# A linear-attention layer and two expert layers on one core: another order for products, weight decoding and attention pieces

## Chip, cores and metric

The kernel runs on one core of a Trainium2 chip. The metric is the device time of one execution, in microseconds (us), as the median of several runs. The engines are named as the profile names them: PE (TensorE, matmuls; PEld is its weight loads), DVE (VectorE), ACT (ScalarE), POOL (GpSimd) and SP (the queue that issues most transfers). Each works through its own instructions in the order in which they were written; they wait for each other by semaphores.

## Reference

Three layers follow each other. The first is a gated linear attention with a state per head (batch 4, 8 heads, 768 positions, 48 wide); the other two are dense layers on its output, with 3072 tokens of 384 numbers.

```
for t in range(S):                       # attention, per batch b and head h
    cur = einsum('bhd,bhe->bhde', u * k[t], v[t])
    y[t] = einsum('bhd,bhde->bhe', r[t], state + cur)
    state = w[t][..., None] * state + einsum('bhd,bhe->bhde', k[t], v[t])
h = x @ w_in;  g = h * clip(h + 3, 0, 6) / 6;  x = g @ w_out       # d_ff 2048
out = ((x @ w_a) * (x @ w_b)) @ w_out2                             # d_ff 1536
```

## The kernel before, in words

The 768 positions are cut into six blocks of 128. A **unit** is one block of one batch: units 0 to 23, four to a block, so units 12 to 23 are blocks 3 to 5 (counted from 0). The attention of a unit is a row of small pieces, each with a letter: on DVE the scans `z`, `c`, `s` over the decays, then `k` (r and k scaled by them); on PE the transposes `T` (copied out by ACT, `t`) and the products `A` (masked on DVE, `m`); the products `K`, which the state update `e`, `f`, `h` on DVE takes; the output `Y`, added up on DVE (`x`); and the transposes `X`, which `H` on ACT and `L` on DVE split into a high and a low part for the next layer. POOL prepares two products `d` per unit, DVE reduces them (`o`), POOL applies them (`O`).

The first dense layer goes over the blocks in **steps** of one weight tile `f` (16 to a block). Step s has one group of nine matmuls `h` (`L1_pe`), and on ACT and DVE `relu`, the product `mul`, the high part `gh` and the low part `gl` (`L1_relu`, `L1_mul`, `L1_high`, `L1_low`); two steps later nine matmuls into `x2a` (`L2_pe`). Blocks 0 and 1 are computed in two halves of eight tiles each, so that steps 8 to 15 are block 1's first half, 16 to 23 block 0's second, 24 to 31 block 1's second. Where a half ends, ACT and DVE copy the three `x2a` banks out (`x2e`), and the next half's first `x2a` product needs these banks. Later layers (`L3_pe`, `L4_pe`, matmuls `ab` and `oa`) follow in the same manner.

Weights come as raw 64-bit words and are **decoded** on the core, a tile of 128x768 at a time: ACT scales the high and the low word (`w_scale_h`, `w_scale_l`), DVE shifts and sets signs (`w_shift`, `w_sign`), POOL adds the halves (`w_add`), and then ACT writes the high part and DVE the low part (`w_split`, `w_high`, `w_low`). Raw tiles have two buffers: the load of a tile waits until POOL has added the tile two before.

Nothing plans the order: it is written out. `run` goes through the steps; in each it issues the attention's vector pieces that are due (`att_ew`), the step's matmuls and vector work, the decoding, and last the attention's PE pieces (`att_pe`). Which piece is due in which step stands in `CFG`: `off` and `second` give a unit's first step n0, and `stage` the steps after it. PSUM has eight banks; attention takes 5, 6, 7 in rotation:

```
    def att_bank(kind, n):
        if ring["use"]:
            i = ring["use"].pop(0)
        else:
            i = (5, 6, 7)[ring["i"] % 3]
            ring["i"] += 1
```

`T`, `A` and `X` take one bank each, `K` and `Y` two.

Of the kernel before, what the change touches and what calls it, by code (L numbers as in the profile page):

```python
# [36 lines left out]

CFG = {
    "off": (0, 3, 6, 9),
    "stage": (0, 1, 2, 3, 4, 5, 0, 2),  # L40
    "second": (17, 20, 23, 26),
    "dec": (8, 9, 11, 12, 14, 15, 18, 19),
    "late": (-16, -14, -12, -10, -8, -6, -4, -2, -1, 0, 1, 2, 3, 4, 5, 6, 7, 8),
    "heat": 13,
    "pool": (
# [27 lines left out]
def rwkv_moe_kernel(ctx: ExitStack, tc: tile.TileContext, rkw, nat, vst, wall, ub, ud, cst, out):  # L73
# [304 lines left out]
    def att_ew(n, stage):  # L378
        j = units[n][0]
        for a in {  # L380
            0: "zcs", "d0": "d", "d1": "oO", 1: "ku" if j else "k", 2: "tm",
            3: "efh" if j < NBLK - 1 else "ef", "x": "x", 5: "HL",
        }.get(stage, ""):
            atom[a](n)

    def att_pe(n, stage):
        for a in {1: "TA", 2: "K", 3: "Y", 4: "X"}.get(stage, ""):
            atom[a](n)

    def heat(k, s):  # L390
# [57 lines left out]
    def w_dec(i):  # L448
        if wide:
            w_scale_l(i)  # L450
            w_shift(i)
            w_sign(i)
            for q in range(2):
                w_add(i, q, nc.gpsimd)
# [69 lines left out]

    def L1_ew(s):
        L1_relu(s)
        L1_mul(s)

    def L1_ew2(s):
        L1_high(s)  # L530
        L1_low(s)

# [79 lines left out]
    def L4_pe(s):  # L612
        j, f = divmod(s, NF2)
        if f == 0:
            acc2[j] = [bank(i, None, f"oa{j}_{i}") for i in (0, 1, 2, 5)]
        ph, pl = G.pop(("b", s))
        w = W[NF1 + NF2 + f // 2]
        c = (f % 2) * 384
        wh, wl = w[:, 0, c:c + 384], w[:, 1, c:c + 384]
        last = f == NF2 - 1  # L620
        seq = [(b, lt, rt) for b in range(B) for lt, rt in ((ph, wh), (ph, wl))] + [(b, pl, wh) for b in range(B)]
        if s == NBLK * NF2 - 1:
            seq.sort(key=lambda x: x[0])
        for b, lt, rt in seq:
            nc.tensor.matmul(  # L625
                out=acc2[j][b][:, 0:384], lhsT=lt[:, b * 128:(b + 1) * 128], rhs=rt,
                start=(f == 0 and rt is wh and lt is ph), stop=(last and lt is pl),
            )
        for b in range(B):
            o = acc2[j][b][:, 0:384]  # L630
            if f == NF2 - 1:
                if b < 3:
                    e = ap_.tile([128, 3 * DM], F32, name=f"oe{j}_{b}", tag="nat", bufs=3)
                else:
                    e = ap_.tile([128, NP * 112], F32, name=f"oe{j}_{b}", tag="kt", bufs=1)
# [188 lines left out]
    def run(at, first, ew, fast):  # L824
        lag, end = [max(first - 1, 0), 0], NA + NBLK * NF2 - 1
        for s in range(first, end + 1):
            act = at.get(s, [])
            sb = s - NA
            for n, sg in act:
                ew(n, sg)  # L830
            if 0 <= s < NA:
                L1_pe(s)
            elif 0 <= sb < NBLK * NF2:
                L3_pe(sb)
            if 0 <= s < NA:
                L1_ew(s)
                L1_ew2(s)
            elif 0 <= sb < NBLK * NF2:
                L3_ew(sb)
            w_step1(s)  # L840
            w_step(s)
            while lag[0] <= min(s - 2, NA - 1):
                L2_pe(lag[0])
                lag[0] += 1
# [52 lines left out]
    with tc.manual_schedule():  # L897
# [90 lines left out]
```

## Time and profile before

| what | value |
|---|---|
| runs shown | 1016.33, 1019.26, 1019.84 us; median 1019.26 |
| profiled execution | 1015.68 us, its span on the core 1013.9 us |
| PE busy | 993.1 us (98%) |
| DVE, ACT, POOL busy | 587.8 (58%), 345.7 (34%), 122.1 us (12%) |
| mean granted TensorE clock | 0.990 of full speed |

The profiled execution is the one that the traces show; it is a little faster than the three runs. A busy share is a mean over stages: PE is full for most of the time, and the few places where it is not are named in the rows below.

### The profile page before, as it was taken

Reading aid. Unit: us, or ns where it says so; the run is one execution under the profiler, and the core shown is the slowest. Engines: PE = TensorE matmul, PEld = TensorE weight load, DVE = VectorE, ACT = ScalarE, POOL = GpSimd, SP = SyncE. Lnnn points to the kernel's source line nnn. Section 1 sums busy time; section 2 is a strip of 40 time slices with the busy share of each in tenths; the row PEclk is TensorE's granted clock in tenths of the full one; section 3 lists DMA queues with packets and bytes.
Section 4 is the critical chain, followed back from the end, with each engine's and each line's share of the span. In section 5 each row is a group of like instructions: output and inputs, shape, how many; then the busy total and the mean of one; then the engine's idle time right before and its main releaser. Section 6 shows DMA issues by size and latency. Waiting matters only on the chain.

```text
span 1013.9 us, 16923 instructions
## 1 busy us (share of the span) xinstructions
PE 993.1 (98%) x7146; PEld 817.2 (81%) x7146; DVE 587.8 (58%) x916; ACT 345.7 (34%) x578; POOL 122.1 (12%) x119
## 2 busy tenths in 40 slices
PE   9999988999999999999999999999999999999997
PEld 5777766787878777777888888888888888888886
DVE  7997787757656765663677673444444444444222
ACT  4464653333223323232566552222222222222211
POOL 1230323111211120210222330000000000000000
PEclk9999989999999999999999999999999999999999
DMA  7362532332231321220243440110110110110001
GB/s 289 132 236 71 209 102 102 118 127 71 87 103 55 103 87 63 95 102 1 94 155 125 159 164 1 56 42 22 65 41 23 64 44 23 63 42 14 32 1 35
DMA packets 30037, 86.64 MB, mean 85 GB/s; under 512 B 3456, under 2 KB 10880, under 8 KB 29952
## 3 DMA queue, kind: packets, MB, share of 16 engines
q1 hardware_dynamic: 29664, 85.37, 24.5%
q8 instruction: 58, 0.95, 0.4%
q14 instruction: 27, 0.22, 0.1%
q10 hardware_dynamic: 288, 0.10, 0.0%
HBM read 74.45 MB, written 11.01 MB: 84 GB/s over the span
## 4 chain that ended last, share of the span: by engine, by line
PE 89%; DVE 6%; DMA 2%; issue 2%; ACT 1%; SPq 0%; DVEq 0%; ACTq 0%
PE ab L474 30%; PE h L474 19%; PE x2a L543 18%; PE oa L625 15%; PE A L272 2%; PE Y L339 2%; DMA rkw<-in_rkw_dram 1%; PE K L294 1%; DVE raw L435 1%; PE T L251 1%; PE X L356 1%; DVE w L464 1%; DVE zp L184 1%; DVE rkw L206 1%; DVE t L513 1%
## 5 line engine op out<-in xcount | busy, mean ns | idle before, releaser
L474 PE MATMUL ab<-xh_b,w 128*128 128x512 f32 x864 | 225.6, 396 | 0.0
L474 PEld LDWEIGHTS ab<-xh_b,w 128*128 128x128 f32 x864 | 161.7, 188 | 33.2
L543 PE MATMUL x2a<-gh,w 128*128 128x512 f32 x576 | 156.7, 403 | 6.2 <-ACT x2e L562 5.5
L603 DVE TENSOR_TENSOR ta<-ab,ta 128x512 f32<-128x512 f32 x72 | 49.7, 691 | 187.9 <-PE ab L474 187.8
L474 PE MATMUL h<-xh_a,w 128*128 128x512 f32 x576 | 157.7, 409 | 0.6 <-ACT xh_a L364 0.6
L543 PEld LDWEIGHTS x2a<-gh,w 128*128 128x128 f32 x576 | 108.9, 191 | 34.4 <-ACT x2e L562 6.3
L509 ACT ACTIVATE t<-h,half 128x512 f32<-128x512 f32 x96 | 65.9, 686 | 181.8 <-PE h L474 181.7
L474 PEld LDWEIGHTS h<-xh_a,w 128*128 128x128 f32 x576 | 105.0, 190 | 25.0 <-ACT xh_a L364 0.8
L474 PE MATMUL ab<-xl_b,w 128*128 128x512 f32 x432 | 124.4, 396 | 0.0
L625 PE MATMUL oa<-w,ph 128*128 128x384 f32 x576 | 113.7, 338 | 0.0
L513 DVE SCALAR_TENSOR_TENSOR t<-t,h 128x512 f32<-128x512 f32 x96 | 65.3, 680 | 79.2 <-ACT t L509 78.8
L522 DVE TENSOR_TENSOR gl<-t,gh 128x512 fp32r<-128x512 f32 x96 | 74.9, 780 | 60.6 <-ACT gh L517 60.6
L625 PEld LDWEIGHTS oa<-w,ph 128*128 128x128 f32 x576 | 103.2, 188 | 6.0
L606 ACT CAST ph<-ta 128x512 fp32r<-128x512 f32 x72 | 44.7, 621 | 160.8 <-DVE ta L603 160.8
L602 ACT COPY ta<-ab 128x512 f32<-128x512 f32 x72 | 42.1, 585 | 164.7 <-PE ab L474 164.7
L474 PEld LDWEIGHTS ab<-xl_b,w 128*128 128x128 f32 x432 | 81.4, 188 | 20.1
L517 ACT CAST gh<-t 128x512 fp32r<-128x512 f32 x96 | 59.5, 620 | 106.4 <-DVE t L513 106.4
L442 POOL TENSOR_TENSOR wa<-wa,raw 128x384 int32<-128x384 int32 x60 | 65.2, 1106 | 198.5 <-DVE raw L435 152.5
L543 PE MATMUL x2a<-gl,w 128*128 128x512 f32 x288 | 86.8, 401 | 0.0
L474 PE MATMUL h<-xl_a,w 128*128 128x512 f32 x288 | 83.3, 397 | 0.0
L607 DVE TENSOR_TENSOR pl<-ta,ph 128x512 fp32r<-128x512 f32 x72 | 54.0, 750 | 49.4 <-ACT ph L606 49.4
L543 PEld LDWEIGHTS x2a<-gl,w 128*128 128x128 f32 x288 | 55.0, 191 | 13.5
(86 smaller groups left out, 1023.0 us busy)
## 6 DMA issues: line engine op xcount, KB each, us to landing
raw<-in_wall_dram SPq DMA_DIRECT2D x34, 768.0 KB, 4.3
rkw<-in_rkw_dram SPq DMA_DIRECT2D x21, 772.5 KB, 4.9
nat<-in_nat_dram SPq DMA_DIRECT2D x16, 576.0 KB, 3.8
cw<-in_rkw_dram SPq DMA_DIRECT2D x24, 260.5 KB, 2.7
x2d<-x2e SPq DMA_DIRECT2D x18, 256.0 KB, 2.1
x2r<-x2d SPq DMA_DIRECT2D x18, 256.0 KB, 3.1
out_dram<-oe SPq DMA_DIRECT2D x24, 192.0 KB, 2.0
vs<-in_vst_dram SPq DMA_DIRECT2D x22, 192.0 KB, 5.0
```

The lines of the kernel that those rows point to most:

```text
L442: eng.tensor_tensor(out=a[:, c], in0=a[:, c], in1=t[:, c, 0], op=ALU.add)
L474: nc.tensor.matmul(out=o, lhsT=lt, rhs=rt, start=(i == 0), stop=(i == 3 * n - 1))
L509: nc.scalar.activation(out=t, in_=hb[s], func=ACTF.Relu, bias=half, scale=1.0 / 6.0)
L513: nc.vector.scalar_tensor_tensor(out=t, in0=t, scalar=1.0, in1=hb.pop(s), op0=ALU.min, op1=ALU.mult)
L517: nc.scalar.copy(out=gh, in_=G["t", s])
L522: ve(f"l{s}").tensor_tensor(out=gl, in0=G.pop(("t", s)), in1=G[s][0].bitcast(F32), op=ALU.subtract)
L543: nc.tensor.matmul(out=acc1[i][k][:, c0:c1], lhsT=w[:, e, 384 + k * 128:512 + k * 128], rhs=rt, start=(first and e == 0 and rt is gh), sto ...
L602: nc.scalar.copy(out=t, in_=a)
L603: nc.vector.tensor_tensor(out=t, in0=bb, in1=t, op=ALU.mult)
L606: nc.scalar.copy(out=gh, in_=t)
L607: nc.vector.tensor_tensor(out=gl, in0=t, in1=gh.bitcast(F32), op=ALU.subtract)
L625: nc.tensor.matmul(out=acc2[j][b][:, 0:384], lhsT=lt[:, b * 128:(b + 1) * 128], rhs=rt, start=(f == 0 and rt is wh and lt is ph), stop=(la ...
```

## The change

It does six things.
1. In the first dense layer, DVE's product `mul` stands ahead of the shift of a weight tile, ACT's scaling of the high word stands between `relu` and `gh`, and the shift between `mul` and `gl`.
2. The tiles 8 to 15 are decoded in steps 8, 9, 10, 12, 13, 14, 16, 17 (before: 8, 9, 11, 12, 14, 15, 18, 19), and up to step 23 each is split one step after its decoding and not two.
3. The scans of unit 8, and in blocks 3 to 5 those of the second to fourth unit of a block, are issued behind the step's product and not ahead of it.
4. In blocks 3 to 5 a unit's `Y` stands one step later, in the step of the next unit's `T` and `A`, and its `X` in the step of the next unit's `K`. The PE pieces of such a step are sorted T, t, Y, A, K, X.
5. `d` of a unit is prepared earlier: two steps in block 2, one in blocks 3 to 5.
6. At the end, the last output tile is copied and sent in two halves by DVE with SP and by ACT, the first of the four goes through ACT's queue, and the flag that decides on the general path is read three steps after it is made, not behind the last output.

```
-    "stage": (0, 1, 2, 3, 4, 5, 0, 2),
+    "stage": (0, 1, 2, 3, 3, 4, 4, 5, 0, 2),
+    "merged": (0, 1, 2, 3, 4, 5, 5, 6, -1, 2),
-    "dec": (8, 9, 11, 12, 14, 15, 18, 19),
+    "dec": (8, 9, 10, 12, 13, 14, 16, 17),
...
+    MERGED = range(12, len(units))
...
-    def att_pe(n, stage):
-        for a in {1: "TA", 2: "K", 3: "Y", 4: "X"}.get(stage, ""):
+    def att_pe(act):
+        seq = [(a, n) for n, sg in act for a in {1: "TtA" if n in MERGED else "TA", 2: "K", 3: "Y", 4: "X"}.get(sg, "")]
+        if any(n in MERGED for a, n in seq):
+            seq.sort(key=lambda x: "TtYAKX".index(x[0]))
+        for a, n in seq:
             atom[a](n)
...
     def L1_ew(s):
         L1_relu(s)
+        w_step1(s)
         L1_mul(s)
-
-    def L1_ew2(s):
+        w_step1b(s)
         L1_high(s)
         L1_low(s)
...
+                if end and b == B - 1:
+                    c = DM // 2
+                    nc.vector.tensor_copy(out=e[:, 0:c], in_=o[:, 0:c])
+                    nc.sync.dma_start(out=out[r0:r0 + 128, 0:c], in_=e[:, 0:c])
+                    nc.scalar.copy(out=e[:, c:DM], in_=o[:, c:DM])
+                    nc.scalar.dma_start(out=out[r0:r0 + 128, c:DM], in_=e[:, c:DM])
+                    continue
...
+    def w_step1b(s):
+        if wide:
+            for i in wdue(s):
+                w_shift(i)
...
-        while pend and pend[0][0] <= s - 2:
+        while pend and pend[0][0] <= s - (1 if s < F0 + NF1 else 2):
...
+            behind = [x for x in act if fast and x[1] == 0 and (x[0] == FIRST_N or x[0] in MERGED and x[0] % 4)]
             for n, sg in act:
-                ew(n, sg)
+                if (n, sg) not in behind:
+                    ew(n, sg)
...
+            if fast and sb == CHECK + 3:
+                chk["good"] = nc.values_load(chk["flag"][0:1, 0:1], min_val=0, max_val=128)
             w_step2(s)
-            for n, sg in act:
-                att_pe(n, sg)
+            for n, sg in behind:
+                ew(n, sg)
+            att_pe(act)
```

**ACT, steps 9 and 10.** `t9` is `relu` of step 9, `raw9` the scaling of tile 9, `w8` the high part of tile 8, `x2e` the copies of the banks. Before:

```order
L509 ACTIVATE t9_1447<-h9_1437,half_85 128x512
L517 CAST gh9_1450<-t9_1447 128x512
L417 ACTIVATE raw9_1435<-raw9_1435 128x768
L562 COPY x2e0_1464<-x2a0_0_929 128x512
L562 COPY x2e0_1464<-x2a0_2_931 128x512
L426 ACTIVATE raw9_1435<-raw9_1435 128x768
L509 ACTIVATE t10_1489<-h10_1479,half_85 128x512
L517 CAST gh10_1492<-t10_1489 128x512
L461 CAST w8_1496<-wa8_1430 128x768
```

With the change:

```order
L513 ACTIVATE t9_1447<-h9_1437,half_85 128x512
L422 ACTIVATE raw9_1435<-raw9_1435 128x768
L521 CAST gh9_1453<-t9_1447 128x512
L465 CAST w8_1457<-wa8_1425 128x768
L566 COPY x2e0_1469<-x2a0_0_929 128x512
L566 COPY x2e0_1469<-x2a0_2_931 128x512
L431 ACTIVATE raw9_1435<-raw9_1435 128x768
L513 ACTIVATE t10_1492<-h10_1482,half_85 128x512
L422 ACTIVATE raw10_1480<-raw10_1480 128x768
L521 CAST gh10_1498<-t10_1492 128x512
```

The high part of tile 8 has moved ahead of the copies, and a scaling ahead of each `gh`; tile 10 is scaled in step 10.

**DVE, steps 17 and 18**, where the first half of block 1 ends and unit 8 begins. `t17` is the product of step 17, `zp8` the two scans of unit 8, `rkw8` its `k`. Before:

```order
L184 SCALAR_TENSOR_TENSOR zp8_1718<-rkw8_1511,ones_rev_87 128x520
L192 TENSOR_SCALAR pc8_1720<-zp8_1718 128x8
L193 RECIPROCAL seed_88<-pc8_1720 128x8
L197 SCALAR_TENSOR_TENSOR zp8_1718<-rkw8_1511,seed_88 128x519
L513 SCALAR_TENSOR_TENSOR t17_1736<-t17_1736,h17_1726 128x512
L522 TENSOR_TENSOR gl17_1741<-t17_1736,gh17_1739 128x512
L464 TENSOR_TENSOR w13_1743<-wa13_1682,w13_1743 128x768
L560 COPY x2e1_1755<-x2a1_1_1500 128x512
L206 TENSOR_TENSOR rkw8_1511<-rkw8_1511,zp8_1718 128x1024
```

With the change:

```order
L517 SCALAR_TENSOR_TENSOR t17_1742<-t17_1742,h17_1732 128x512
L436 TENSOR_SCALAR wa15_1746<-raw15_1730 128x768
L526 TENSOR_TENSOR gl17_1750<-t17_1742,gh17_1748 128x512
L468 TENSOR_TENSOR w14_1752<-wa14_1711,w14_1752 128x768
L564 COPY x2e1_1764<-x2a1_1_1506 128x512
L440 SCALAR_TENSOR_TENSOR raw15_1730<-raw15_1730 128x768
L186 SCALAR_TENSOR_TENSOR zp8_1775<-rkw8_1523,ones_rev_87 128x520
L194 TENSOR_SCALAR pc8_1777<-zp8_1775 128x8
L195 RECIPROCAL seed_88<-pc8_1777 128x8
L199 SCALAR_TENSOR_TENSOR zp8_1775<-rkw8_1523,seed_88 128x519
L208 TENSOR_TENSOR rkw8_1523<-rkw8_1523,zp8_1775 128x1024
```

The scans have moved from ahead of the product to behind the copy and the sign of tile 15, and `k` now stands directly behind them.

**DVE, steps 38 and 39**, unit 14 in block 3, as in all second to fourth units of blocks 3 to 5. `t38` is the product of step 38, `gl38` its low part, `zp14` the scans, `rkw14` the `k` for which `T` of unit 14 waits at the end of step 39, `nat13` the `x` of unit 13. Before:

```order
L184 SCALAR_TENSOR_TENSOR zp14_2927<-rkw14_2807,ones_rev_87 128x520
L192 TENSOR_SCALAR pc14_2929<-zp14_2927 128x8
L193 RECIPROCAL seed_88<-pc14_2929 128x8
L197 SCALAR_TENSOR_TENSOR zp14_2927<-rkw14_2807,seed_88 128x519
L513 SCALAR_TENSOR_TENSOR t38_2945<-t38_2945,h38_2935 128x512
L522 TENSOR_TENSOR gl38_2950<-t38_2945,gh38_2948 128x512
L349 TENSOR_TENSOR nat13_2407<-Y0_13_2961,nat13_2407 128x4x48
L349 TENSOR_TENSOR nat13_2407<-Y1_13_2962,nat13_2407 128x4x48
L206 TENSOR_TENSOR rkw14_2807<-rkw14_2807,zp14_2927 128x1024
```

With the change:

```order
L517 SCALAR_TENSOR_TENSOR t38_2939<-t38_2939,h38_2929 128x512
L526 TENSOR_TENSOR gl38_2944<-t38_2939,gh38_2942 128x512
L186 SCALAR_TENSOR_TENSOR zp14_2955<-rkw14_2860,ones_rev_87 128x520
L194 TENSOR_SCALAR pc14_2957<-zp14_2955 128x8
L195 RECIPROCAL seed_88<-pc14_2957 128x8
L199 SCALAR_TENSOR_TENSOR zp14_2955<-rkw14_2860,seed_88 128x519
L208 TENSOR_TENSOR rkw14_2860<-rkw14_2860,zp14_2955 128x1024
L311 TENSOR_TENSOR sp14_0_2962<-st2_95,pc14_2957 112x192
L517 SCALAR_TENSOR_TENSOR t39_2974<-t39_2974,h39_2964 128x512
L526 TENSOR_TENSOR gl39_2979<-t39_2974,gh39_2977 128x512
```

The scans have moved from ahead of `t38` to behind `gl38`. On PE, before, step 38 ends with `Y` of unit 13, and step 39 with `X` of unit 13 and `T`, `A` of unit 14; now step 38 ends with its `x2a` products alone, step 39 with `T` of 14, `Y` of 13, `A` of 14, and step 40 with `K` of 14 and `X` of 13.

## Rows read from the trace of the kernel before

**Rows 1.** Waits of PE: waiting engine and line, releaser, us in total, times, longest.

```profile
PE x2a L543 <- ACT x2e L562: 5.5, 2, 3.7
```

**Rows 2.** Stretches: us, busy time of each engine, granted clock (PEclk), DMA.

```profile
147.84:153.20 5.36, 5.36 (x17) 3.72 (x19) 4.31 (x8) 3.30 (x6) 0.00 (x0) 0.50 0.77 275
173.75:177.10 3.35, 3.35 (x17) 2.62 (x14) 2.71 (x4) 1.21 (x3) 0.44 (x1) 0.52 0.00 0
```

**Rows 3.** Timeline, steps 8 to 10: start, us, engine, instruction, [idle before <- releaser].

```profile
103.19 0.91 ACT L417 ACTIVATE raw<-raw 128x768 f32<-128x768 f32 x1 [0.68 <-DMA raw<-in_wall_dram]
...
105.99 1.99 POOL L442 TENSOR_TENSOR wa<-wa,raw 128x384 int32<-128x384 int32 x2 [24.19 <-DVE raw L435]
...
107.85 1.05 ACT L562 COPY x2e<-x2a 128x512 f32<-128x512 f32 x2
...
108.47 2.79 PE L543 MATMUL x2a<-gh,w 128*128 128x512 f32 x6 [1.80 <-ACT x2e L562]
```

**Rows 4.** Timeline, steps 17 and 18, DVE and PE.

```profile
141.57 2.05 DVE L184 TENSOR_TENSOR_SCAN zp<-rkw,ones_rev 128x520 f32<-128x520 f32 x1
...
144.10 1.24 DVE L197 TENSOR_TENSOR_SCAN zp<-rkw,seed 128x519 f32<-128x519 f32 x1
...
147.84 3.19 PE L543 MATMUL x2a<-gh,w 128*128 128x512 f32 x6 [3.67 <-ACT x2e L562]
...
152.10 0.95 PE L251 MATMUL T<-cst_sb,rkw 112*128 112x112 f32 x4
```

**Rows 5.** Timeline, end of step 21, DVE and PE.

```profile
171.06 1.22 DVE L206 TENSOR_TENSOR rkw<-rkw,zp 128x1024 f32<-128x1024 f32 x1
...
172.38 0.57 PE L251 MATMUL T<-cst_sb,rkw 112*128 112x112 f32 x4 [3.17 <-issue]
```

**Rows 6.** Page, DMA issues: transfer, queue, count, KB each, median us to landing.

```profile
raw<-in_wall_dram SPq DMA_DIRECT2D x34, 768.0 KB, 4.3
```

**Rows 7.** Timeline of PE in block 3's steps.

```profile
228.61 1.57 PE L474 MATMUL h<-xh_a,w 128*128 128x512 f32 x6
...
232.83 1.57 PE L474 MATMUL h<-xh_a,w 128*128 128x512 f32 x6
...
248.04 0.33 PE L339 MATMUL Y<-sp,rkw 48*64 48x48 f32 x8
...
249.12 1.67 PE L474 MATMUL h<-xh_a,w 128*128 128x512 f32 x6
...
253.76 0.55 PE L251 MATMUL T<-cst_sb,rkw 112*128 112x112 f32 x4
...
255.32 1.67 PE L474 MATMUL h<-xh_a,w 128*128 128x512 f32 x6
```

**Rows 8.** Timeline of ACT and DVE behind the `h` that starts at 255.32.

```profile
257.79 0.69 ACT L509 ACTIVATE t<-h,half 128x512 f32<-128x512 f32 x1 [2.86 <-PE h L474]
...
259.24 0.62 ACT L517 CAST gh<-t 128x512 fp32r<-128x512 f32 x1 [0.76 <-DVE t L513]
...
259.89 0.69 DVE L522 TENSOR_TENSOR gl<-t,gh 128x512 fp32r<-128x512 f32 x1 [0.69 <-ACT gh L517]
```

**Rows 9.** Timeline of DVE and ACT, scans, `k`, state scale and `t` of one unit.

```profile
244.91 1.23 DVE L184 TENSOR_TENSOR_SCAN zp<-rkw,ones_rev 128x520 f32<-128x520 f32 x1
...
246.62 1.24 DVE L197 TENSOR_TENSOR_SCAN zp<-rkw,seed 128x519 f32<-128x519 f32 x1
...
250.26 1.21 DVE L206 TENSOR_TENSOR rkw<-rkw,zp 128x1024 f32<-128x1024 f32 x1
...
251.39 0.35 DVE L309 TENSOR_TENSOR sp<-st,pc 112x192 f32<-112x192 f32 x1
...
254.40 0.53 ACT L261 COPY kt<-T 128x448 f32<-128x448 f32 x1
```

**Rows 10.** Instructions of line 905, the reading of the flag: ns, start in us.

```profile
L905 PEldq TENSOR_LOAD <-chk_flag x1: 487/487/487, 1004.0 to 1004.0; - x1
...
L905 SPq TENSOR_LOAD <-chk_flag x1: 565/565/565, 1008.5 to 1008.5; - x1
```

More of the change, by code (lines that the diff above doesn't have):

```diff
@@ L380, in att_ew @@
         for a in {
-            0: "zcs", "d0": "d", "d1": "oO", 1: "ku" if j else "k", 2: "tm",
-            3: "efh" if j < NBLK - 1 else "ef", "x": "x", 5: "HL",
+            0: "zcs", "d0": "d", "d1": "oO", 1: "ku" if j else "k", 2: "m" if n in MERGED else "tm",
+            "e": "efh" if j < NBLK - 1 else "ef", "x": "x", 5: "HL",
         }.get(stage, ""):
             atom[a](n)
-    def att_pe(n, stage):
-        for a in {1: "TA", 2: "K", 3: "Y", 4: "X"}.get(stage, ""):
+    def att_pe(act):
[3 more added lines that the diff above has]
+        for a, n in seq:
             atom[a](n)
@@ L450, in w_dec @@
             w_scale_l(i)
-            w_shift(i)
             w_sign(i)
@@ L637, in L4_pe @@
                 r0 = b * S + j * 128
+                end = s == NBLK * NF2 - 1
+                if end and b == B - 1:
[5 more added lines that the diff above has]
+                    continue
                 if b % 2 == 0:
@@ L641, in L4_pe @@
                     nc.vector.tensor_copy(out=e, in_=o)
-                nc.sync.dma_start(out=out[r0:r0 + 128, :], in_=e)
+                (nc.scalar if end and b == 0 else nc.sync).dma_start(out=out[r0:r0 + 128, :], in_=e)
     at = {}
-    STAGES = (0, 1, 2, 3, "x", 4, 5, "d0", "d1")
+    STAGES = (0, 1, 2, "e", 3, "x", 4, 5, "d0", "d1")
     for n in range(FIRST_N, len(units)):
@@ L648, in rwkv_moe_kernel @@
         n0 = CFG["second"][i] if j == 2 else NF1 * (j - 1) + CFG["off"][i]
-        a, b, c, d, x, h, d0, d1 = (n0 + k for k in CFG["stage"])
+        p = [n0 + k for k in CFG["merged" if n in MERGED else "stage"]]
         if j == 2:
-            h = max(h, F0 + NF1)
-        for sg, s in zip(STAGES, (a, b, c, d, x, h - 1, h, d0, d1)):
+            p[7] = max(p[7], F0 + NF1)
+            p[6] = p[7] - 1
+            p[8] -= 2
+        for sg, s in zip(STAGES, p):
             at.setdefault(s, []).append((n, sg))
     for s in at:
-        at[s].sort(key=lambda x: (x[0], {"d1": 3.5, "d0": 0.5, "x": 3.7}.get(x[1], x[1])))
+        at[s].sort(key=lambda x: (x[0], {"e": 2.5, "d1": 3.5, "d0": 0.5, "x": 3.7}.get(x[1], x[1])))
     wdec = {}
@@ L836, in run @@
                 L1_ew(s)
[L837 to L840, printed above, removed]
+            elif s < 0:
+                w_step1(s)
+                w_step1b(s)
+            else:
+                if 0 <= sb < NBLK * NF2:
+                    L3_ew(sb)
+                w_step1(s)
             w_step(s)
+            if s >= NA:
+                w_step1b(s)
             while lag[0] <= min(s - 2, NA - 1):
@@ L904, in rwkv_moe_kernel @@
         run(at, F0, att_ew, True)
-        good = nc.values_load(chk["flag"][0:1, 0:1], min_val=0, max_val=128)
-        with tc.If(good < 128):
+        with tc.If(chk["good"] < 128):
             general_attention()
```

## Prediction

> **What bounds the kernel now.** The page's busy times come first: PE is busy for 993.1 of 1013.9 us, so an edit is worth what it takes from PE's own row or from the few places where PE stands still. The waits of PE name the largest, the first `x2a` product of a half, which waited for ACT's copies of the banks [rows 1]. The timeline gives the places. There are three stops, all in steps 10 to 21: 1.80 us at 108.47 [rows 3], 3.67 at 147.84 [rows 4] and 3.17 at 172.38 [rows 5]. After each the granted clock is at its lower level, 1.2 GHz, for a while: 0.50 of full speed over 5.36 us after the second, 0.52 over 3.35 us after the third [rows 2]. So the second stop costs 3.67 + 5.36 / 2 = 6.3 us and the third 3.17 + 3.35 / 2 = 4.8 us; the first at least 1.80 + 2.79 - 1.57 = 3.0, by its first six matmuls beside six at full clock [rows 3, 7]. From there to the end PE is full. In blocks 3 to 5 a step without attention takes 232.83 - 228.61 = 4.22 us, and an `h` behind attention pieces shows 1.67 us for its first six matmuls where a plain one shows 1.57: returning from small pieces costs 0.10 us [rows 7]. The kernel has little to win: the stops of blocks 0 and 1, about 14 us, the 0.10s, and the tail.
>
> **Blocks 3 to 5, second to fourth unit (9 units).** This is where the sum is decided. `T` of such a unit comes two steps behind the `h` of its first step; call the start of that `h` zero. PE reaches `T` after a step behind attention pieces, 4.32 us, and a plain one, 4.22: at 8.54 [rows 7]. On the other side DVE must finish `k`, and the scans that `k` needs now stand behind `gl` of the first step. `relu` starts at 257.79 - 255.32 = 2.47, `gl` 2.10 later at 4.57, and ends at 5.26 [rows 8]. From the first scan's start to the end of the second are 246.62 + 1.24 - 244.91 = 2.95 us: 8.21. `k` takes 1.21: 9.42 [rows 9]. The only row in which `T` waited for `k` has `k` end at 171.06 + 1.22 = 172.28 and `T` start 0.10 later [rows 5]. So `T` starts at 9.4 to 9.5, and PE stands still for **0.95 us**; the lower figure holds if each instruction starts a little before its forerunner's end, as `k` and the state scale do (251.39 is 0.08 before 250.26 + 1.21 [rows 9]). Before, the scans ran while PE made the first `h`, and no `T` of this stretch shows a wait.
>
> A second wait follows. A step's pieces now take banks in the order T, Y, Y, A out of three, so `A` gets `T`'s bank and must wait for `t`, ACT's copy. `t` stands behind `gh` of the same step, whose product stands on DVE behind `k` and the state scale. From the end of `k` at 9.42: state scale 0.35 [rows 9], then from the product's start to `gh` 259.24 - 257.79 - 0.69 = 0.76 us, `gh` 0.62 [rows 8], `t` 0.53 [rows 9]: 11.7, or 11.4 with the small overlaps. PE meanwhile does `T`, 0.55, and `Y`, 249.12 - 248.04 = 1.08 [rows 7]: 9.5 + 1.6 = 11.1. So `A` waits for 0.3 us (0.2 to 0.6). Before, `X`, `T`, `A` stood in three different banks. Together 0.95 + 0.3 = 1.25 us per unit, times nine: **+11.3 us**. The bounds are +7 (the overlaps cut the first wait to 0.8 and `A` finds its bank free) and +14. Behind PE's wait nothing else is late: `h` of the next step has its bank, and the next unit's chain starts from its own `h`, so the wait does not grow and is not made up.
>
> The rows show `T` and the following `h` without a wait bracket where the banks rotate [rows 7]. The Trainium skill (Perfetto Trace Analysis, Matmuls) says that independent groups should rotate through different PSUM banks, so that the copy of one runs beside the next group's matmuls; this change breaks that for `T` and `A`. By the rule alone `A` would wait for all of `t`, less the `Y` between them, which gives the same sum to within the bounds above.
>
> **What the grouping gives back.** A block's attention stood in 13 groups on PE and now in 10, so three returns of 0.10 us are saved per block: **-0.9 us** in three blocks, -1.8 if entering a group costs as much. No matmul is removed.
>
> **Blocks 0 and 1.** The edits go both ways here.
> First stop: the copies started at 107.85 [rows 3]; now the high part of tile 8 stands ahead of them, and it needs POOL's adds. These ended at 105.99 + 1.99 = 107.98, and they come about 0.5 us later, since ACT waits until 103.19 for the raw tile [rows 3] with `gh` now behind that wait. High part 0.9 (the row of the same size on ACT, 0.91 [rows 3]): copies at 109.3 or so, **+1.4 us**.
> Second stop: unit 8's scans no longer hold up the product, so the copies could come earlier. But `k` of unit 8 now follows the copy, the sign, and both scans: the scans took 144.10 + 1.24 - 141.57 = 3.77 us beside POOL [rows 4], `k` 1.22 [rows 5], together 4.99, while PE has one half step of 2.11 us to do. From those alone `T` waits for 2.9 us, and for up to 4.3 with the copy and the sign at 0.69 each (the nearest row, `gl` [rows 8]). The stop moves from `x2a` to `T`; I take 4.0, **+0.3 us**.
> Three tiles in four steps: a raw tile's load starts when POOL has added the tile two before and takes 4.3 us to land [rows 6]. From there ACT's two scalings and a high part (0.9 each), `gh` 0.6, DVE's sign about 0.7 and the adds 1.99 make 10.3 us for two tiles, 5.2 a tile. The steps ask for one every 4 x 4.22 / 3 = 5.6. So there is no slack to make up the first stop's lateness, and ACT, with `gh` behind the scaling, hands each late load on to the copies of the next half: 0 to 5 us later. I take 3.2, half of the range and some clock with it, **+3.2 us**.
> Third stop: decoding is done by then and no sign stands in front of unit 9's scans, so `T` of unit 9 finds `k` done: 3.17 + 1.7 = 4.8 us gone, **-4.9 us** with rounding.
> The sum of these four is 1.4 + 0.3 + 3.2 - 4.9 = 0, with bounds of -5 and +5.
>
> **Tail.** The flag's reading leaves SP's path behind the last transfer, 0.57 us [rows 10], and half an output tile is copied in less time, 0.2 at a guess from its halved width: **-0.8 us**, between 0 (the last landing sets the end) and -1.5. In its new place the reading takes PE's sequencer 0.49 us; before, that was done at 1004.0 while matmuls ran until 1007 [rows 10], so it hides behind queued matmuls, at 0 to +0.5.
>
> **Sum.** 0 + 11.3 - 0.9 - 0.8 = **+9.6 us**. The profiled execution took 1015.68, which gives 1025.3. It is the fastest of the four executions shown; their mean is 1017.8, and a median of new runs should lie near that plus the sum: **1027.4 us**.
>
> **Rivals.**
> A. The wait at `T` doesn't form: PE stays behind DVE. It would need `k` 0.9 us earlier, which is the point from which it decides. Against it: each link is a row, and DVE takes nothing out of order in any of them. Price: 11.3 us, leaving about -1.7: 1016, no change.
> B, the other side. The stops of blocks 0 and 1 vanish altogether, because the loads land early enough for the copies to be out when PE comes, and `T` of unit 8 finds `k` done. The point is the landing of tiles 13 and 15 before their step's `relu` ends. Price: the second stop's 6.3 and the third's 4.8 go, with nothing put in their place: -11.1, with +11.3 - 0.9 - 0.8: -1.5, so 1016, not slower. Against it: 4.99 us of DVE work stand between the copies and `T`, and PE has 2.11.
> C. The nine waits bring the clock down. Each spell like the third stop's costs 1.7 us, nine of them 15 us more: 1043. Against it: the stops that the clock followed were of 1.80 us and more [rows 3 to 5], these are 0.95 and 0.3. The Trainium skill (TensorE: Matmul & The Clock Gate, A second HAM failure mode) describes this: frequent small idles between matmul groups make the clock swing. No row here shows it for idles as short as these.
>
> **Chances.** Forecast, +4 to +16 us: 0.64. A 0.14, B 0.10, C 0.12. About 5 us, 0.5%, is what a measurement of this kernel can tell from no change. A and B end near 1016 with spreads of some 5 us, so they give most of "same" and half of "faster"; the forecast's lower edge lies at "same". That makes faster 0.11, same 0.18, slower 0.71. The likeliest case's own range is 1020 to 1034. For 8 in 10 the range reaches into A and B below and into part of C above: 1013 to 1038.
>
> **What would show it.** In the new profile, PE rows `T` of units 13, 14, 15, 17, 18, 19, 21, 22, 23 with an idle of about 0.9 us released by `k`, and `A` behind with 0.2 to 0.6 released by `t`; rounds of three steps in block 3 longer by about 1.1 us; the first stop longer, a stop at unit 8's `T`, none at unit 9's. If `T` shows no idle there, the main term is wrong (A); if the granted clock shows half speed in blocks 3 to 5, C is right.

## The result, and the profile after

| what | before | after |
|---|---|---|
| median of the runs | 1018.28 us (4 runs, 1016.33 to 1019.84) | 1031.88 us (4 runs, 1030.88 to 1032.02) |
| profiled execution, its span | 1015.68, 1013.9 us | 1030.88, 1029.1 us |
| PE busy | 993.1 us (98%) | 995.3 us (97%) |
| mean granted TensorE clock | 0.990 | 0.985 |

The changed kernel is slower: the ratio of the times is 1.0135, with a 95% interval of 1.0115 to 1.0155. PE does the same work in a longer span, so the question is where it stands still. The first view is the waits of PE after the change (microseconds in all, times, longest); it answers to [rows 1].

```profile
PE T L253 <- issue: 10.9, 10, 3.8
PE x2a L547 <- ACT x2e L566: 7.3, 2, 3.8
...
PE A L274 <- ACT kt L263: 2.3, 9, 0.3
```

`T` waits ten times where it waited once, and `A` nine times where it never did. "issue" is how the page names `T`'s releaser; the rows below show that it is `k`. They are the timeline of block 3 after the change, for the second unit: PE first, then DVE, then ACT (start, length, instruction, and in brackets the idle before it; this idle is called the bracket below). They answer to [rows 7 to 9].

```profile
248.77 1.67 PE L478 MATMUL h<-xh_a,w 128*128 128x512 f32 x6
...
256.61 0.87 PE L547 MATMUL x2a<-gl,w 128*128 128x512 f32 x3
258.27 0.57 PE L253 MATMUL T<-cst_sb,rkw 112*128 112x112 f32 x4 [0.79 <-issue]
...
259.62 0.30 PE L341 MATMUL Y<-vs,am 64*64 64x48 f32 x8
260.17 1.15 PE L274 MATMUL A<-rkw 48*64 48x64 f32 x32 [0.25 <-ACT kt L263]
...
253.34 0.69 DVE L526 TENSOR_TENSOR gl<-t,gh 128x512 fp32r<-128x512 f32 x1 [0.69 <-ACT gh L521]
253.95 1.24 DVE L186 TENSOR_TENSOR_SCAN zp<-rkw,ones_rev 128x520 f32<-128x520 f32 x1
...
256.94 1.23 DVE L208 TENSOR_TENSOR rkw<-rkw,zp 128x1024 f32<-128x1024 f32 x1
...
259.59 0.53 ACT L263 COPY kt<-T 128x448 f32<-128x448 f32 x1
```

The scans start behind `gl` at 253.95, so `k` ends at 256.94 + 1.23 = 258.17, and `T` starts 0.10 later. `t` ends at 259.59 + 0.53 = 260.12, and `A`, in the same bank, starts 0.05 later.

The stages are compared by the starts of `h` rows, which mark a place in the program: the `h` of steps 7, 16, 24 and 32, and the first `ab`, with which the later layers begin. The stretch from step 32 to the first `ab` is called blocks 3 to 5, since the attention of these blocks lies in it. The bounds of the windows are those starts (columns: stretch, its length, PE busy with the count, granted clock, share of the DMA engines, GB/s). Before:

```profile
91.34:133.47 42.13, 39.76 (x224) 0.96 0.47 169
133.47:186.32 52.85, 46.01 (x413) 0.90 0.23 83
...
228.61:547.19 318.58, 318.58 (x2709) 1.00 0.25 86
```

After the change, and below it the stretch of low clock behind the second `x2a` stop:

```profile
93.54:138.15 44.61, 39.86 (x223) 0.96 0.44 160
138.15:191.46 53.31, 46.01 (x412) 0.87 0.24 83
...
233.76:561.85 328.09, 318.66 (x2710) 1.00 0.25 83
...
151.65:165.30 13.65, 9.15 (x50) 0.50 0.37 131
```

So the profiled pair differs by +2.20 us up to step 7, where no edit acts, +2.48 in steps 7 to 15 (44.61 - 42.13), +0.46 in steps 16 to 23, nothing in steps 24 to 31, **+9.51 in blocks 3 to 5**, nothing in the later layers, and +0.54 from PE's last matmul to the end (7.08 against 6.54): 15.2 us in all, which is 1030.88 - 1015.68. Blocks 3 to 5 lose at a granted clock of 1.00, the 2.4 GHz level, and PE's own rows take as long as before (318.66 for 318.58): these are waits alone.

The rows of steps 9 to 21 after, on PE and then POOL and ACT, answer to [rows 3 to 5].

```profile
112.68 0.74 PE L547 MATMUL x2a<-gh,w 128*128 128x512 f32 x2 [3.81 <-ACT x2e L566]
...
152.39 3.19 PE L547 MATMUL x2a<-gh,w 128*128 128x512 f32 x6 [3.53 <-ACT x2e L566]
...
160.62 0.98 PE L253 MATMUL T<-cst_sb,rkw 112*128 112x112 f32 x4 [3.77 <-issue]
...
179.06 0.55 PE L253 MATMUL T<-cst_sb,rkw 112*128 112x112 f32 x4
...
108.99 2.29 POOL L447 TENSOR_TENSOR wa<-wa,raw 128x384 int32<-128x384 int32 x2 [24.99 <-DVE raw L440]
...
111.31 0.83 ACT L465 CAST w<-wa 128x768 fp32r<-128x768 f32 x1 [1.15 <-POOL wa L447]
112.05 1.06 ACT L566 COPY x2e<-x2a 128x512 f32<-128x512 f32 x2
```

The first stop grew from 1.80 to 3.81 us, the second stayed (3.53 for 3.67), a new one came at unit 8's `T`, and unit 9's `T` no longer waits.

### The profile page after: what moved, and what is told of

Its sections match the earlier page's. It is cut to its first block, busy times and chain, and to the rows that moved or that the text cites. A ratio compares the mean times of both kernels' runs of the same rounds, so it can differ in the third digit from the quotient of the medians.

```text
span 1029.1 us, 16948 instructions
## 1 busy us (share of the span) xinstructions
PE 995.3 (97%) x7146; PEld 819.2 (80%) x7146; DVE 589.0 (57%) x916; ACT 346.8 (34%) x579; POOL 123.4 (12%) x119
## 4 chain that ended last, share of the span: by engine, by line
PE 79%; DVE 9%; issue 4%; DMA 3%; ACT 3%; POOL 1%; SPq 0%; ACTq 0%; POOLq 0%; DVEq 0%
PE ab L478 29%; PE h L478 15%; PE oa L629 15%; PE x2a L547 14%; DMA raw<-in_wall_dram 2%; PE A L274 2%; DVE zp L199 2%; DVE t L517 1%; DVE zp L186 1%; POOL wa L447 1%; PE K L296 1%; PE Y L341 1%; DVE raw L440 1%; DVE gl L526 1%; DMA rkw<-in_rkw_dram 1%
```

## The experiments

The time up to step 7 changes from run to run though no edit changes the work of PE, ACT, DVE or POOL there: the `h` of step 7 starts between 91.34 and 98.27 us in the fourteen profiles. Medians of few runs therefore scatter by some 3 us, and the main measure is the table, worked out as above: microseconds longer than the profiled execution of before, stage by stage, and the time from the end of PE's last matmul row to the end of the span (read to 0.1 us).

| kernel | steps 7 to 15 | 16 to 23 | blocks 3 to 5 | last matmul to end | median, runs |
|---|---|---|---|---|---|
| changed | +2.48 | +0.46 | +9.51 | 7.08 | 1031.88, 4 |
| e1_blocks01_only | +3.14 | +0.37 | 0.0 | 6.79 | 1022.66, 10 |
| e2_scans_ahead | +2.19 | +0.44 | -1.51 | 6.97 | 1020.03, 10 |
| e3_blocks35_only | +0.17 | -0.42 | +9.52 | 6.38 | 1025.86, 4 |
| e4_t_twice | +3.20 | +0.30 | +15.66 | 6.16 | 1038.62, 4 |
| e5_stops_freed | +0.52 | +1.59 | 0.0 | 6.37 | 1019.58, 10 |
| e6_split_behind_copies | +1.49 | +3.21 | +9.51 | 7.23 | 1032.06, 2 |
| e7_old_decode_steps | +3.12 | -2.17 | +9.47 | 7.26 | 1029.84, 2 |
| e8_freed_and_scans_ahead | +0.09 | +1.63 | -1.64 | 6.72 | 1018.14, 10 |
| e9_fewer_tiles_at_ends | -3.77 | -6.20 | -1.65 | 6.66 | 1007.54, 4 |
| e10_same_old_order | -3.67 | -1.17 | -1.64 | 6.42 | 1011.63, 4 |
| e11_copies_first | -3.77 | -6.18 | -1.66 | 6.40 | 1009.02, 4 |
| e12_with_new_tail | -3.77 | -5.05 | -1.61 | 7.08 | 1010.13, 4 |

The kernel before, run beside them, had medians of 1018.1 to 1019.5. The first two columns have a scatter of their own. The changed kernel, e1, e2 and e4 do the same in steps 7 to 15 and differ by 1.0 us there. e9 and e12 do the same in steps 16 to 23 and differ by 1.2: e9 keeps a granted clock of 1.00 there behind idles of 1.06 and 1.72 us, e12 shows 0.96 over the same steps behind 1.04 and 1.70. Blocks 3 to 5 repeat to 0.05 us among kernels with the same order there.

### Which part carries the loss (e1 to e4)

**e1_blocks01_only**, against the changed kernel:

```
-    MERGED = range(12, len(units))
+    MERGED = ()
```

> The changed kernel with blocks 3 to 5 as before; the new order of blocks 0 and 1 and the new tail stay. Theory (the nine waits at T and A, 7.1 + 2.3 = 9.4 us in the trace, are a real price and nothing makes them up): 1031.9 - 9.4 = 1022.5 us, no idle of T in blocks 3 to 5. Rival 1 (the waits lie beside something else that ends as late, so that the new order of blocks 0 and 1 carries the loss): 1030 to 1032. Rival 2 (the loss lies in blocks 3 to 5 alone): 1018 to 1019.

Measured: 1022.66 us, ratio to before 1.0036 (1.0019 to 1.0053). `T` waits once, at unit 8 (4.0 us). The theory holds, both rivals fall.

**e3_blocks35_only**, the complement: the new groups of blocks 3 to 5 and the tail stay, and the decoding, the split, the order inside a step, unit 8's scans and `d` of block 2 are as before.

```
-    "dec": (8, 9, 10, 12, 13, 14, 16, 17),
+    "dec": (8, 9, 11, 12, 14, 15, 18, 19),
...
-            behind = [x for x in act if fast and x[1] == 0 and (x[0] == FIRST_N or x[0] in MERGED and x[0] % 4)]
+            behind = [x for x in act if fast and x[1] == 0 and x[0] in MERGED and x[0] % 4]
```

> The kernel before with the new order of blocks 3 to 5 and the new tail alone; the order, the decoding and the stops of blocks 0 and 1 as before. Theory: 1018.3 + 9.4 + 0.5 = 1028.2 us, with the nine idles at T (0.8 us) and A (0.25 us). Rival 1 (blocks 0 and 1 carry the loss): 1018 to 1020. Rival 2 (everything lies in blocks 3 to 5): 1031 to 1032.

Measured: 1025.86 us, ratio 1.008 (1.0055 to 1.0104), blocks 3 to 5 longer by 9.52 us as in the changed kernel; the median is 2.3 us below the expectation, within the scatter of the start. So two parts lose, each by itself, and stage by stage they add up.

**e2_scans_ahead** takes away the one suspected cause:

```
-            behind = [x for x in act if fast and x[1] == 0 and (x[0] == FIRST_N or x[0] in MERGED and x[0] % 4)]
+            behind = [x for x in act if fast and x[1] == 0 and x[0] == FIRST_N]
```

> The changed kernel with the scans of the second to fourth units of blocks 3 to 5 back ahead of the step's product; unit 8's stay behind. Theory (k is late because the scans stand behind gl): the idle of T, 7.1 us in all, is gone, and the idle of A stays near 0.25 us each, since t still stands behind gh: 1031.9 - 7.1 = 1024.8 us. Variant: A's idle goes too, 1022.5. Rival (the scans then hold up the product, gh and gl, and x2a two steps later, or h, waits in their place): 1029 to 1032 with idle rows at x2a in blocks 3 to 5.

Measured: 1020.03 us, ratio 1.0016 (0.9999 to 1.0033). `T`'s idles in blocks 3 to 5 are gone, and `A` waits only four times, 0.9 us in all. Its PE timeline shows a unit whose `T` and `A` are free:

```profile
255.43 0.86 PE L547 MATMUL x2a<-gl,w 128*128 128x512 f32 x3
256.13 0.55 PE L253 MATMUL T<-cst_sb,rkw 112*128 112x112 f32 x4
...
257.46 0.30 PE L341 MATMUL Y<-vs,am 64*64 64x48 f32 x8
257.58 1.13 PE L274 MATMUL A<-rkw 48*64 48x64 f32 x32
```

Here the price of a stop can be read from start to start, which the idle in brackets understates. From the last `x2a` row to `T` are 0.70 us without the stop and, in the changed kernel, 258.27 - 256.61 = 1.66 with it: 0.96 us for a bracket of 0.79. From the last `Y` row to `A` are 0.12 without and 260.17 - 259.62 = 0.55 with it: 0.43 for 0.25. The round of three steps that holds this unit, steps 36 to 38 from `h` to `h`, took this long before, in the changed kernel and in e2:

```profile
249.12:265.83 16.71, 16.71 (x196) 1.00 0.29 95
...
253.10:270.86 17.76, 16.72 (x190) 1.00 0.29 90
...
251.92:268.25 16.33, 16.33 (x190) 1.00 0.30 98
```

So the two stops cost 17.76 - 16.33 = 1.43 us a unit, 12.9 in nine and not the 9.4 of the brackets, and the grouping gives back 16.71 - 16.33 = 0.38 a unit, 3.4 in nine; the other rounds agree to 0.07. That is why e2 came out lower than expected.

**e4_t_twice** doubles the other cost:

```
+        for _ in range(2 if n in MERGED and n % 4 else 1):
             nc.scalar.copy(out=kt[0:r], in_=u["ktp"][0:r, 0:448].rearrange("p (a m) -> p a m", m=112))
```

> The changed kernel with ACT's copy t of T made twice, one behind the other, for the nine units. Theory (A stands in T's bank and waits until t has read it): A waits longer by one copy, 0.53 us nine times, 1031.9 + 4.8 = 1036.7 us, idle of A 0.8 us each. Rival (A waits for something else that ends at about the same time, its operands or its bank's earlier reader): 1031.9 and the same idle.

Measured: 1038.62 us. `A` waits 7.4 us in nine idles, 0.81 to 0.83 each for 0.25 before, and blocks 3 and 4 grow by 1.55 us each, 0.52 per unit: one copy of `t`. So `A` does wait for its bank's reader, and the rival falls. Block 5 grew by 1.5 us more, and its rows (timeline, then windows) show why:

```profile
456.65 0.54 PE L253 MATMUL T<-cst_sb,rkw 112*64 112x112 f32 x4 [0.73 <-issue]
...
459.10 1.88 PE L275 MATMUL A<-rkw 48*64 48x64 f32 x32 [0.83 <-ACT kt L264]
```

```profile
458.60:462.30 3.70, 3.20 (x35) 0.59 0.84 249
```

Behind idles of 0.73 and 0.83 us the granted clock read 0.59 over 3.70 us, so most of that stretch ran at 1.2 GHz. It happened once in nine such pairs, and never behind the 0.79 and 0.25 of the changed kernel.

### Where blocks 0 and 1 lose (e6, e7)

**e6_split_behind_copies**, against the changed kernel:

```
-            w_step(s)
+            if s != F0 + 1:
+                w_step(s)
...
                 L2_pe(lag[0])
                 lag[0] += 1
+            if s == F0 + 1:
+                w_step(s)
```

> The changed kernel with the high and low part of tile 8 behind the copies of the x2a banks in step 9. Theory (the first stop grew from 1.80 to 3.81 us because the copies stand behind the high part, which waits for POOL's adds): the copies start about 1.9 us earlier, the first stop is 1.9 us, and 16 steps of blocks 0 and 1 are 2 to 3 us shorter: 1029 to 1030. Rival (the stop is as long since ACT is late from the scaling of tile 9 and gh): the stop stays at 3.5 to 3.8 us and the time at 1031.9.

Its PE timeline:

```profile
109.99 0.73 PE L547 MATMUL x2a<-gh,w 128*128 128x512 f32 x2 [1.85 <-ACT x2e L566]
111.79 1.20 PE L547 MATMUL x2a<-gh,w 128*128 128x512 f32 x4 [1.07 <-DVE x2e L564]
...
152.09 3.18 PE L547 MATMUL x2a<-gh,w 128*128 128x512 f32 x6 [3.82 <-ACT x2e L566]
```

The high part did hold up ACT's copies: 3.81 became 1.85, though DVE's copy was then late by 1.07. But 1032.06 us, of two runs, is no gain. In steps 7 to 15 PE stands still as long as in the changed kernel (43.62 - 38.83 = 4.79 us for 44.61 - 39.86 = 4.75): what it wins at the first stop, it waits for a few steps later, at `x2a` for `gh` (0.47) and at `h` for DVE's product (0.83). The 1.0 us won there is the clock, 1.00 for 0.96. Steps 16 to 23 lost 2.75, 1.1 of it idle and 1.7 in PE's own rows, at a clock of 0.85 for 0.87. This fits a pace that the decoding sets and not the copies; e7 tests it.

**e7_old_decode_steps**:

```
-    "dec": (8, 9, 10, 12, 13, 14, 16, 17),
+    "dec": (8, 9, 11, 12, 14, 15, 18, 19),
```

> The changed kernel with tiles 8 to 15 decoded in the old steps (8, 9, 11, 12, 14, 15, 18, 19), the rest as changed. Theory (three tiles in four steps make ACT late, which is why x2a of step 18 still waits 3.53 us though unit 8's scans no longer stand ahead of the product; and the end of decoding before unit 9's scans took the third stop away): x2a's second stop is below 1 us, T of unit 8 still waits about 4 us, T of unit 9 waits again for about 3 us, the first stop stays 3.8 us; blocks 0 and 1 about as long as changed, 1030 to 1033. Rival (the second x2a stop has another cause and stays at 3.5 us): 1034 to 1037.

```profile
114.75 3.19 PE L547 MATMUL x2a<-gh,w 128*128 128x512 f32 x6 [4.02 <-ACT x2e L566]
...
156.12 0.57 PE L253 MATMUL T<-cst_sb,rkw 112*128 112x112 f32 x4 [2.28 <-issue]
...
177.40 0.57 PE L253 MATMUL T<-cst_sb,rkw 112*128 112x112 f32 x4 [3.17 <-issue]
```

With two tiles in three steps again the second `x2a` stop is gone, unit 9's `T` waits again, and unit 8's waits for 2.28 rather than the expected 4. Steps 16 to 23 are 2.6 us shorter than changed, and the median of two runs is 1029.84. The theory holds but for unit 8's `T`. So the density of the decoding kept the second stop alive after unit 8's scans had left its way.

### Can the stops be taken away (e5, e8 to e12)

**e5_stops_freed**, against the kernel before; the scans of units 8 and 9 (`a` is their step) also stand behind the step's work, and the split behind the copies:

```
-    "dec": (8, 9, 11, 12, 14, 15, 18, 19),
+    "dec": (8, 10, 11, 12, 14, 15, 16, 18),
...
+        a = {8: 13, 9: 19}.get(n, a)
```

> The kernel before with only this changed: tiles 8 to 15 decoded in steps 8, 10, 11, 12, 14, 15, 16, 18, so that none falls in the steps whose end copies the x2a banks out (9 and 17); a tile's high and low part behind those copies; the scans of unit 8 behind the step's work of step 13 and those of unit 9 behind that of step 19. Theory (each of the three stops of blocks 0 and 1 is ACT or DVE holding work that need not stand there, and costs its idle and half of the slow stretch behind it, 3.0 + 6.3 + 4.8 us): 1018.4 - 14 = 1004 us, and no x2a or T idle over 0.5 us in steps 9 to 22. Rival 1 (the raw tiles, one step apart, then come too late, and the stops move to other steps): 1012 to 1018. Rival 2 (the slow stretches are not caused by the stops and stay): 1018.4 - 8.6 = 1010.

Measured: 1019.58 us, ratio 1.0008 (0.9993 to 1.0023). A miss: the stops moved, as rival 1 says, though the time lies just above its range. PE, ACT and SP around step 17, and PE in step 20:

```profile
153.10 1.22 PE L543 MATMUL x2a<-gh,w 128*128 128x512 f32 x2 [5.15 <-ACT x2e L562]
...
147.17 0.90 ACT L417 ACTIVATE raw<-raw 128x768 f32<-128x768 f32 x1 [1.24 <-DMA raw<-in_wall_dram]
...
152.47 1.06 ACT L562 COPY x2e<-x2a 128x512 f32<-128x512 f32 x2
...
119.01 28.13 SPq L409 DMA_DIRECT2D raw<-in_wall_dram  x5
...
171.00 0.65 PE L339 MATMUL Y<-sp,rkw 48*64 48x48 f32 x4 [1.79 <-DVE st L320]
```

Unit 9's `T` waits no more, but in step 20 `Y` of unit 8 waits 1.79 us for the state update; the first stop is 1.45 + 0.73 us in two pieces (1.80 before), and `h` waits twice for DVE's product, 1.42 and 0.64 us at 136.24 and 141.36. Tiles in neighbouring steps also wait for their loads: SP takes 28 us to issue five, since each needs the buffer of the tile two before. ACT stands at the scaling for 1.24 us until 147.17 with all later work behind it, and the second stop grew from 3.67 to 5.15.

**e8_freed_and_scans_ahead** puts those blocks 0 and 1 beside the new groups of blocks 3 to 5 with every scan ahead of the product, and the old tail.

> Blocks 0 and 1 as in the kernel with the stops freed; blocks 3 to 5 in the new grouping, but with every scan ahead of the product; the old tail. Theory (the two add up): 1004 - 1.5 = 1002.5 us, below both kernels. Rival (the grouping and the freed blocks disturb each other, or the stops stay): 1010 to 1018.

Measured: 1018.14 us, ratio 1.0003 (0.9991 to 1.0016), a miss that the rival had named: the -1.6 us of blocks 3 to 5 came, the stops stayed (5.1 us at the second).

**e9_fewer_tiles_at_ends**, against the changed kernel; it has e2's scans and the old tail as well:

```
-    "dec": (8, 9, 10, 12, 13, 14, 16, 17),
+    "dec": (9, 10, 12, 13, 15, 16, 18, 20),
...
+        if n == FIRST_N:
+            p[0] = 13
...
-        while pend and pend[0][0] <= s - (1 if s < F0 + NF1 else 2):
+        while pend and pend[0][0] <= s - (2 if raw.get("parts") or s >= F0 + NF1 else 1):
...
         wnext[0] = F0
         w_ahead()
+        w_ahead()
```

> The changed kernel with its product first, but tiles 8 to 15 decoded in steps 9, 10, 12, 13, 15, 16, 18, 20 (never more than two in three steps, none in the steps 8 and 17), each split two steps later and its raw tile loaded two tiles ahead; unit 8's scans behind the work of step 13, all others ahead of the product; the old tail. Theory (the denser decoding made the copies of step 17 late, a raw tile that had not landed held up ACT in step 8, and the scans in step 17 made T of unit 8 wait; with all three gone and the shift in the gap between product and low part, blocks 0 and 1 have room): no stop over 1 us in steps 8 to 22, 10 to 11 us off these steps and 1.5 us off blocks 3 to 5: 1018.1 - 12 = 1006 us (1003 to 1010). Rival (the stops only move again, as with the stops freed): 1015 to 1020.

Measured: **1007.54 us, ratio to before 0.989 (0.9864 to 0.9916)**, faster than both kernels. Its windows by steps 7 to 15 and 16 to 23, then PE and DVE around step 18:

```profile
93.14:131.50 38.36, 37.79 (x223) 1.00 0.49 180
131.50:178.15 46.65, 42.46 (x412) 1.00 0.29 99
```

```profile
143.27 0.73 PE L547 MATMUL x2a<-gh,w 128*128 128x512 f32 x2 [1.06 <-ACT x2e L566]
145.73 1.20 PE L547 MATMUL x2a<-gh,w 128*128 128x512 f32 x4 [1.72 <-DVE x2e L564]
...
145.00 0.68 DVE L564 COPY x2e<-x2a 128x512 f32<-128x512 f32 x1
```

The first stop is gone, the clock stays at 1.00, and 10 us are won in these seventeen steps. The expected "no stop over 1 us" is missed at step 18 (1.06 and 1.72). Which of the new steps, the later split, the earlier load and unit 8's earlier scans does how much was not tried.

**e10_same_old_order** is e9 with the order inside a step as before:

```
         L1_relu(s)
-        w_step1(s)
         L1_mul(s)
-        w_step1b(s)
         L1_high(s)
```

> The kernel of the run with fewer tiles at the ends, with the order inside a step as before: the shift ahead of the sign behind low part, ACT's first scaling behind gh. Theory (the product first is worth something here: with the shift in DVE's gap of 0.69 us between product and low part a step with decoding fits into PE's step; without it DVE falls behind by half a microsecond a tile and the copies of step 17 are late): a stop of 2 to 4 us at x2a in step 18, 1012 to 1015 us. Rival (the order inside a step is worth nothing, only the steps of the decoding count): 1006, as in the other run.

```profile
145.00 1.22 PE L546 MATMUL x2a<-gh,w 128*128 128x512 f32 x2 [3.49 <-ACT x2e L565]
```

Measured: 1011.63 us, ratio 0.9931 (0.9906 to 0.9955). The stop of 2 to 4 us is there, and steps 16 to 23 are 5.0 us longer than in e9, 2.1 of them PE's own rows at a clock of 0.93 for 1.00; the medians differ by 4.1. The order inside a step, product first, is an edit of the change and is worth that where decoding leaves it room.

**e11_copies_first** is e9 with the split behind the copies in step 17 too (the edit of e6, at `2 * F0 + 1`).

> The kernel of the run with fewer tiles at the ends, with the split of a tile behind the copies of the x2a banks in step 17 too. Theory (what was left of the second stop, 1.06 + 1.72 us, is DVE's copy behind the low part, 1.76 us beside POOL): DVE's copy starts about 1.7 us earlier, the stop is 1 us or less, 1007.5 - 2 = 1005.5 us. Rival (k of unit 8, which now stands behind the low part, makes T wait instead): 1007 to 1008 with an idle at T of step 18.

```profile
152.26 0.57 PE L253 MATMUL T<-cst_sb,rkw 112*128 112x112 f32 x4 [1.17 <-issue]
```

Measured: 1009.02 us, ratio 0.9887 (0.9851 to 0.9923), not told apart from e9. The rival is right: the stop shrank to 0.33 and 0.78, and unit 8's `T` waits instead.

**e12_with_new_tail** is e9 with the tail of the change (`end` and the early reading of the flag back).

> The kernel of the run with fewer tiles at the ends, with the new tail (the flag read three steps behind the sum, the last tile copied in halves by DVE and ACT, two of the last stores on ACT's queue). Theory (the tail is worth nothing: from PE's last matmul to the end of the span the kernels with the new tail took 6.2 to 7.3 us and those with the old one 6.4 to 6.7): 1007.5 us, 6.2 to 7.3 us from the last matmul to the end. Rival (the new tail saves 0.8 us, which the other parts hid): 1006.7, with 5.7 to 6.0 us.

Measured: 1010.13 us, ratio 0.9917 (0.9884 to 0.9949), 7.08 us from the last matmul to the end. The six profiles with the old tail take 6.37 to 6.72, mean 6.52; the eight with the new one 6.16 to 7.26, mean 6.87. The tail saves nothing.

## Why the prediction was right, and where its terms were off

The forecast was 1027.4 us, slower; the median is 1031.88, within the likeliest case's own range. The sum of the terms was +9.6, and without the stretch up to step 7 the profiled pair shows 9.51 + 2.94 + 0.54 = +13.0. The main term was right in mechanism and size; that the sum came so near owes something to luck, as the terms below show.

- **Wait at `T`, 0.95 us: as forecast.** `k` ends 258.17 - 248.77 = 9.40 behind the first `h` (forecast 9.42), `T` starts at 9.50 and would have started at 256.61 + 0.70 - 248.77 = 8.54 (forecast 8.54). The price is 0.96, shown by e2, where the scans alone are moved back. Rival A falls.
- **Wait at `A`, 0.3 us: right mechanism, 0.43.** `t` ends 11.35 behind the first `h` (forecast 11.4 to 11.7). e4 shows that the bank's reader is what counts. The Trainium skill (Perfetto Trace Analysis, Matmuls) asks for rotated banks between independent groups; by e4 the trace agrees, 0.52 us a unit for 0.53 us more of copy.
- **Grouping, -0.9 us: mis-sized.** The round without waits shrank from 16.71 to 16.33, 0.38 a unit, 3.4 us in nine. The term took only the slower first `h` behind a group, 0.10. The stops at 12.9 less 3.4 make 9.5, the measured 9.51. So +11.3 - 0.9 = 10.4 was close because two sizes were off in opposite directions.
- **Blocks 0 and 1, 0 us: two terms mis-sized, +2.9.** The first stop was put at +1.4 for the right reason, the high part ahead of the copies (111.31). Steps 7 to 15 lost 2.48: counted from the `h` of step 8 (97.98 before, 100.17 after), POOL's adds end at 11.11 for 10.00, 1.1 us later and not 0.5, so the copies start 2.0 later, and DVE's copy came another 0.37 late. The step that failed is "the stop moves from `x2a` to `T`": it stayed at `x2a` (3.53) and came at `T` too (3.77 for the forecast 4.0). The drift, a term of +3.2 beside it, is what kept it there, as e7 shows; its size was taken from the middle of a range and not from a row, and the prediction's own 5.2 us a tile against 5.6 left 0.4 of slack where it says that there is none. Together +0.3 + 3.2 were forecast; measured are 3.53 - 3.67 + 3.77 of idle, and 9.15 / 2 = 4.6 us lost at the lower clock for 5.36 / 2 = 2.7 [rows 2], in all +5.5; less the 4.9 of the third stop that is 0.6 for the measured 0.46. The windows say it more simply: PE's own rows take 46.01 us in steps 16 to 23 before and after, and its idle went from 3.67 + 3.17 to 3.53 + 3.77. That the third stop goes, -4.9, was right: unit 9's `T` shows no idle, for 3.17 + 1.7 before [rows 2, 5].
- **Tail, -0.8 us: wrong.** The step that failed is "copied in less time". The timeline of the last tile, PE, DVE, ACT:

```profile
1021.68 0.34 PE L629 MATMUL oa<-w,pl 128*128 128x384 f32 x1
...
1022.06 0.36 DVE L645 COPY oe<-oa 128x192 f32<-128x192 f32 x1 [0.51 <-PE oa L629]
...
1022.45 0.32 ACT L647 COPY oe<-oa 128x192 f32<-128x192 f32 x1 [0.44 <-DVE oe L645]
```

  ACT's half began when DVE's had ended, so the copy was out 1022.77 - 1022.02 = 0.75 us behind PE's last row; before, in one piece, 0.60 (1007.96 - 1007.36). Whether the shared bank or the shared output tile makes ACT wait was not tried. The flag's reading had been hidden behind the last landing, the forecast's lower bound of nothing: it ended at 1008.5 + 0.57 = 1009.1 [rows 10], and the last store landed at 1011.95. The late copy isn't the whole account, though. By the traces the last store lands 4.1 to 4.7 us behind PE's last row in the eight profiles with the new tail, 4.4 to 5.0 in the six with the old (means 4.3 and 4.8); the rest of the span then takes 2.0 to 3.1 us (mean 2.5) for 1.5 to 2.0 (mean 1.8). So the stores won about half a microsecond and the end of the program behind them took 0.8 longer; why it takes longer is open.
- **Rival B** falls with the stops of 3.81 and 3.53. **Rival C** falls for this kernel, at a clock of 1.00 from step 32 to the first `ab`. The Trainium skill (TensorE: Matmul & The Clock Gate, A second HAM failure mode) describes swings from small idles between groups; the trace shows none for 0.79 and 0.25 us, and one in nine pairs in e4, for 0.73 and 0.83.

The medians differ by 13.6 us, 0.6 more than the pair's +13.0; the spread of the start is larger than that.

## What to carry to other kernels

Count an edit of order from both sides: moving work behind an instruction frees that one and makes late whoever needs the work, and the arithmetic on rows (`k` at 9.42 against PE at 8.54) decided it here to a tenth of a microsecond. When a stop is taken away and the time stays (e5, e6, e11), look for the chain that sets the pace behind it, here loads, scaling, sign and adds of the decoding, and thin that out where PE needs the same engines; only then did the first stop go and the others shrink (e9). Test the edits of a bundle one by one, since this one held two good ones, the groups (-1.5 us without the late scans) and the product first (5 us in e10), under two bad ones, the late scans and the denser decoding. Two of its edits were never tried alone: the earlier `d` and the split one step after the decoding.

## What was not expected of the hardware

- A stop of PE cost 0.17 to 0.18 us more here than its bracket says (0.96 for 0.79, 0.43 for 0.25), since rows of neighbouring groups overlap where nothing waits (in e2 the `x2a` row of 255.43 lasts 0.86 us, and `T` starts at 256.13).
- A small DVE instruction can stretch beside POOL by as much as a large one. The limit of the scan on 128x8, 0.17 us alone, took 0.80 in step 17, and `k` 1.83 for 1.23, while POOL was at work (the row of 154.71, and its `d` behind it), in the changed kernel (rows below). Not every one does: DVE's product took 0.68 us at 108.83 with POOL's adds from 108.99 on, as without them.

```profile
155.82 0.80 DVE L194 TENSOR_SCALAR pc<-zp 128x8 f32<-128x8 f32 x1
...
158.69 1.83 DVE L208 TENSOR_TENSOR rkw<-rkw,zp 128x1024 f32<-128x1024 f32 x1
...
154.71 2.84 POOL L447 TENSOR_TENSOR wa<-wa,raw 128x384 int32<-128x384 int32 x2 [3.72 <-DVE raw L440]
```

- The same start, up to the `h` of step 7, took 91.34 to 98.27 us in fourteen profiles, while the 318.6 us of blocks 3 to 5 repeated to 0.05 us among kernels with the same order there. What makes the start differ was not looked into.
- The granted clock answered like stops differently: behind 1.06 and 1.72 us of idle it stayed at 1.00 in e9, behind 1.04 and 1.70 it fell in e12.
